# Three of seven triangular inversions from VectorE to GpSimd, and a new written order, in a delta-rule attention with an MLP mixer

## The chip, the cores and the metric

One core of one Trainium2 chip. The metric is the time of one execution on the device in microseconds, as the median of several runs. Inputs lie in the chip's memory (HBM) at the start, the output at the end.

## The reference

Two blocks in a row, all in fp32. The first is delta-rule attention, a recurrence over 768 positions for each of 4 batches x 8 heads with head dimension 48; the second mixes tokens and then channels with two small MLPs.

```python
# q, k, v: (4, 8, 768, 48), beta: (4, 8, 768)
k_n = k / (norm(k) + 1e-6)
for t in range(768):
    y[t] = q[t] @ state
    state = state + beta[t] * outer(k_n[t], v[t] - k_n[t] @ state)
x = y as (4, 768, 384)                       # heads side by side
h = relu(x.T @ w_tok1) @ w_tok2              # 768 -> 256 -> 768
u = x + h.T
out = u + relu(u @ w_ch1) @ w_ch2            # 384 -> 1536 -> 384
```

## The kernel before

**Units and rounds.** The sequence is cut into chunks of 64 positions, and two chunks make a unit: 6 units a batch, 24 in all (u = 0 to 23), 48 chunks (t = 0 to 47). Inside a chunk the recurrence becomes matrix products once the strictly triangular matrix of key products (times beta) of each head has been turned into the inverse of the identity plus it. The kernel inverts the 32 x 32 diagonal blocks of that matrix on a vector engine and joins the blocks to 64 x 64 with matmuls. Several units are inverted together, so that the 128 partitions hold 128 blocks: round 0 is units 0 to 3, round 1 units 4 and 5, rounds 2 to 5 four units each (6 to 9, 10 to 13, 14 to 17, 18 to 21), round 6 units 22 and 23.

**Jobs.** Every part of the work is a Python generator, a job, that records a few instructions at each step:

- `k`u loads keys and queries, `p`u (prep) makes norms, scales and masks (L497 mask times scale into `mb`, L514 scaled keys, both on GpSimd from u=4 on), `v`u loads the values and scales them (L411, L414 on GpSimd).
- `c`u and `d`u (grams): the key and query products of a unit's two chunks on TensorE (p_g, L440), which VectorE takes out of PSUM with the mask (L443, into `gm`).
- `t`u (to_parts): from u=6 on, four DMAs (L608) write the unit's 32 x 32 blocks to a tile in HBM, `n_dram`, from where `i` loads them in another layout, one block a partition.
- `i`r (invert): step 0 is one load (L655), steps 1 to 30 are one multiply (L661, into `sub`) and one add (L666, into `x`) each, step 31 sets the diagonal to one (L671) and stores the result to `w_dram` (L685).
- `f`u (from_parts): four DMAs (L633) bring a unit's inverted blocks back into `gm`.
- `j`u (join): VectorE transposes a block (L734), TensorE multiplies (p_z L748, p_x L751 and L767), ScalarE takes it out.
- `r`t (recur): the recurrence of a chunk: p_k (L790), rest on VectorE (L797), p_y and p_w (L810, L814), w_t on ScalarE (L820), p_s and p_y (L828, L829), the new state on VectorE (L837). Each chunk needs the state of the one before.
- `m`b (mixer): the MLPs of batch b, most of TensorE's work: p (L986), p_h (L999), p_ut (L1009), p_c (L1066) for batch 0, p_r (L958) for the others, and p_o (L1088).
- `w`n: pieces of the weights, loaded over SP (L271), scaled on ScalarE (L277, L278), shifted on VectorE (L280) and added on GpSimd (L284, unsigned integers); differences of weights on VectorE (L299, and `s`, L899).
- `x`, `z`, `Y`: matmuls of zeros whose results nobody reads, one narrow, one wide, eight small ones.

**Order.** Nothing reorders the instructions of an engine: a string, `order`, says which job makes its next step, and each engine's queue, SP's queue of DMAs too, runs in the order in which the steps were recorded. An engine waits at the head of its queue for semaphores. `i3*2` in the string means two steps of the fourth round's inversion.

**Engines and memories.** PE is TensorE, DVE VectorE, ACT ScalarE, POOL GpSimd. All DMAs are issued from SP. The inversions of all seven rounds run on VectorE.

Of the kernel before, what the change touches and what calls it, by code (L numbers as in the profile page):

```python
# [23 lines left out]
def kernel(  # L24
# [614 lines left out]
    def invert(rnd):  # L639
# [14 lines left out]
        else:  # L654
            nc.sync.dma_start(out=x, in_=xins.pop(rnd)[0:n])  # L655
        yield
        for s in range(1, m - 1):
            w = m - 1 - s
            tmp = work.tile([128, HB * HB // 4], FP32, name="sub")
# [1 line left out]
            nc.vector.tensor_tensor(  # L661
                out=tmp, in0=y[:, :, 0:s, s : s + 1].to_broadcast([n, k, s, w]),
                in1=y[:, :, s : s + 1, s + 1 : m].to_broadcast([n, k, s, w]),
                op=ALU.mult,
            )
            nc.vector.tensor_tensor(  # L666
                out=y[:, :, 0:s, s + 1 : m], in0=y[:, :, 0:s, s + 1 : m], in1=tmp,
                op=ALU.add,
            )
# [492 lines left out]
    order = """
    w10 x*4 z w10*2 z w1*4 k1*3 z k1*3 z b p1 z p1 k0*6 p0*2 b*2 p1 w2 p0*5 p1*2
    w10 p0*2 z w3 w2 c0*3 p0 w3*2 d0*2 w3 c0 p1 c0 d0*3 k2*3 v1 p1*2 w18 k2*2 p1*2
    c1*2 d1 k2 p2*2 c1 t0 d1 c1*2 d1*3 t0 p2*8 c2*2 w2 d2 c2*3 Y d2 w2 k3*6 p3 d2*2
    p3 d2 t1*3 x p3*7 c3 k4*5 k7 w13 w18*2 d3*2 v1*2 v0*2 c3*3 v0 c3 d3*3 t0 p4*2
    t2*3 x t3*2 p4*2 x t3 i0*2 w13 p4*2 w18 w17*2 i0 k4 i0*9 p4 i0*2 p4*2 c4 k8
    c4*3 w13*2 w6*2 k5*2 v0 k6 k5*2 i0*2 d4*2 k5 x z d4*3 c4 z*2 p5*2 k5 t4 p5 h0
    h1 h0 w8*2 h1 Y i0 f0 Y p4 f1 h2*2 p5*3 f0*2 w6 h0*5 k6*5 p6 z f2*2 k8*3 p5 w6
    p5 p3 p5 j0*3 f1*2 h1*5 j0*2 w8*2 w17 f2 h2*3 v0 t4*2 w17 r0*5 p6 h2*2 c5*2 v1  # L1170
    w11*2 j1 p5 k7*2 c5 k7 c5 r0 c5 r0*2 w14*2 v1 w11*2 k7*2 p7 d5*5 r1*5 w14*2
    p6*2 t5 j1 t5*2 r1*2 j1 j2 p7 h3*2 r1*3 p6*3 i1*2 r2*5 k8*2 f3*2 w9 k9*3 j1*2
    v2*2 i1*3 j2*2 r2*2 f3 i1*2 p6*3 w16 v2 w16*3 r2*2 h3 r2 i1 d6 r3*5 i1*2 w9*3
    v2 d6 h3 v2 w0 h3*2 r3 h3 d6*2 w0 d6 j3 c6*5 r3*4 w0 j2 w0 p8*2 j2 r4 p8 r4*4
    k9*3 j3*2 r4*2 i1*2 w24 i1*2 p7*7 r4 c7 r4 r5*5 k10 p9 k10 p9 c7 r4 c7*3 i1
    w5*2 p7 r5*2 w24*3 r5*3 j3*2 i1 r6*4 w26 v3*5 p9 k11 r6 d7*5 w26*3 p8*3 t6*2
    r6*2 w5*2 p8*4 v4*2 t6 i1 r6*3 h5*2 h4*2 k10*2 f4*3 c8*2 k10 p10 w28*2 c8*2 r7
    c8 r7*3 d8*4 p9 d8 w28 h4*5 p9 t6 r7*2 j4 w28 p9*3 r7*2 p9 w7 d9 w7 v4*2 f5*2
    w27*2 w7*2 d9*4 c9*2 f5 c9*3 t7*2 t8 r7*2 t7*2 j4*2 v4 p10*2 h5 r8*3 w29 t8*3
    w29 w27*2 r8*2 w29*3 j4*2 r8 w22*4 t9*4 r8*3 p10 h5*2 k11 p9 r8 h5 r9 h5 j5  # L1180
    r9*4 w4 i2*2 p10 i2*2 v5 i2 v5 w19 m0 r9 k10 j5 p10 i2 p10 v5 i2*2 w15 w4 v5*2
    w4 r9*2 i2 m0 v7 k11 j5 i2 k11*2 r9 v7 j5 p10 i2 r10 v7 i2 w15*2 i2 k12 r10*3
    w15 r10 r9 m0 j5 r10*3 i2*3 r10 p10 d10 c10*3 w25 i2 c10 d10*2 w19 k12 w4 k11
    r11*3 k12*2 w19 k12 i2 r11 r10 m0 r11 i2 r11*2 d10 Y i2*3 r11 w12 r11 i2*2
    k12*3 Y w19 w21 v6 i2 v6 i2*2 m0 i2 k12 i2*2 k12*2 w12 v6 i2*2 Y v6*2 m0*2 v7
    p12*2 m0*2 c10 m0 p11*2 f6 w21 p11 f6*2 m0*2 w12*2 f7*2 m0 f7 w21 p10 m0 p11*2
    d10 w21 m0 p12 m0 j6*2 f6 p11 j6 f8*2 w25 m0 f7 f8 w23 f8 p11 j7*3 w25 p12 m0
    w25*2 r12*2 v7 r12*3 j8*2 w31 r12 t10 w23*2 t10 j8 f9*2 m0 w23 r12 r13 w23 w32
    f9 k12 r13*2 t10*2 r13 f9 p12 p11 w31*3 r12 w30 k13 p11*2 k13 m0 r13*2 d11 k13
    d11 c11*2 r13 w32*3 r13*2 d11 w30 r13 w20*2 c11 k13*2 c11*2 w30*2 r14*2 k13 d11  # L1190
    k13 d11 r14*3 p12*2 w29 m0*4 w20*2 v8 r14 k13 d12 r14 c12 d12 c12 d12 p13 c12
    d12*2 k13*2 r14 p13*2 r14*2 m0 k13*2 v8*2 r15 w23 c12*2 w25 r15*4 p12 p13*2 v8
    w33 t11 j9 m0*2 w31 r15 p13*2 t11 t12 k14*2 m0 k14 m0*2 w31 r15 m0 r15 p13
    r15*2 c13*2 w31 k14*2 d13 c13 t11 d13 c13 d13 r16 d13 r16 c13 k14 d13 w33*2 v8
    w33 w27 k14 w27 t12*3 w33 k14 t13 r16*3 w33 m0*2 j9 w27 m0*2 t11 w25 j9 r16
# [7 lines left out]
    v11*3 r20 j11*2 m0*2 p15*2 k16*2 r20*2 m0 r20 c15 p15 d15*3 c15 j12 v11 p16 k16
    r20 d15 c15 p16*2 r21*2 c15 k16 c15 r21*2 r20 p16 r21 d15 f13 m0 p16*2 s r21*2
    m0 r21*2 j12 v11 r22*2 t14 r22*3 r21 m0 j12 r22*2 k17 p16 d16*2 s*2 c16 r22*2
    k17*3 m0 d16 k17 r22 k17 c16 k17*2 t15 k17*3 d16*2 c16 r23*2 c16*2 p17*3 r23
    p17 r23 t14 p17 k17 v12 r23 m0*2 p17 m0*2 s r23 p17 t14 r23 t15*2 m0*2 s v12
    c17 d17 c17*2 d17 t16 c17*2 d17*2 r23*2 d17 t16 m0*2 s*2 t16*2 m0 t14 v12*3 t15
    s t17 s*2 t17*3 m0*2 f12 m0*2 f13 i4 k18 j13 k18*2 m0*2 i4*3 p17 p16 m0 j13*2
    i4*4 m0*2 k18*2 i4*2 f13 r24*3 k18 r24*2 j13 k18*2 p18*2 k18 p18 r24 i4*2 r24  # L1210
    v14 m0 k18 m0*2 i4*3 m0*2 i4 k18*2 m0 i4 r24 r25*3 p18 r25 i4*2 v14*2 m1*2 v14
    p18 k19 i4 r25 k19 m1*3 k19 r25 m1 r25 i4*3 k19 i4 k19*3 r25 i4 v13*2 i4 v13*2
    i4*3 v13 k19 i4 m1 p18 i4*2 m1 p18 k19 r25*2 m1 k19 m1 p19 m1 r26 j13 p18 d18
    r26*2 d18 k19 r26*2 p19*2 m1*3 k19 r26 m1*3 f14*3 d18 c18*2 d18 r26*3 m1*5 c18
    r27*2 f14 c18 f17 r27*2 r26 r27 m1 p19 d18 j14 v14 m1*2 f15 r27 m1 r27 p19 f16
    j14 c18 f15*2 j14 r27*3 p19 m1*3 j15*2 f17 f16 p19 v15 j15 f16 k20*4 r28*4
    k20*2 m1*3 d19 r28*3 s m1 s k20*4 v15 s*2 r28 c19 d19*3 j16 c19*2 r28*2 d19
    r29*2 p19 c19 f16 k20 r29*2 f17 r29 v15*2 m1*2 k20 p20*2 c19 p20 m1*2 p20 f15
    m1*3 t18 r29 p20 k21 m1 r29 m1*3 p20 m1 k21*4 r29 m1*2 r29*2 p20 k21*3 m1 k21
    m1*3 k21 j16*2 t18 v15 k21 r30*5 k21 m1*3 r30 c20*3 p21*2 c20*2 t18 d20 r30  # L1220
    v16*2 t19 r30*2 p20 p21*2 r30 d20*3 r31*4 d20 r31*3 m1*2 p21*3 t19*3 r31*2 m1*2
# [57 lines left out]
```

## Time and profile before

| | us |
|---|---|
| median of 3 runs | 641.08 (639.05, 641.08, 644.09) |
| the profiled execution | 638.03 |
| its span, from first to last instruction | 636.3 |

| engine | busy us | share of the span | instructions |
|---|---|---|---|
| PE (matmuls) | 606.3 | 95% | 9132 |
| PEld (weight loads, beside PE) | 529.0 | 83% | 9132 |
| DVE | 447.3 | 70% | 1132 |
| ACT | 259.5 | 41% | 631 |
| POOL | 108.7 | 17% | 146 |

An fp32 matmul leaves two records, a transpose one. Rows of groups in the profile give the line, engine, operation, out<-in with partitions x elements and the count; behind the bar stand the busy time in us, the mean ns of one, and the engine's idle time just before them with what ended it. Rows of the timeline give the start in us, the length in us, engine, line, operation, and how many equal ones were merged.

### The profile page before, as it was taken

To read this page: it belongs to the slowest core of one execution; us is meant where nothing else is said; L and a number is where in the kernel's file an instruction comes from. 1 tells how busy PE (TensorE), PEld (TensorE's weight loads), DVE (VectorE), ACT (ScalarE), POOL (GpSimd) and SP (SyncE) were. 2 spreads that over 40 slices of the span, in tenths; PEclk is the share of its full clock that TensorE was granted. 3 is DMA by queue.
4 is the path that set the end of the run, shared out by engine and by line. 5 is a ranking of instruction groups with operands and counts; after the bars stand their busy time and mean duration, and the time that the engine had idled before them with its cause. 6 is when DMAs were issued, how large, how long until landed. Compare 5 with 4: busy or idle time off the path is not lost.

```text
span 636.3 us, 21488 instructions
## 1 busy us (share of the span) xinstructions
PE 606.3 (95%) x9132; PEld 529.0 (83%) x9132; DVE 447.3 (70%) x1132; ACT 259.5 (41%) x631; POOL 108.7 (17%) x146
## 2 busy tenths in 40 slices
...
GB/s 201 131 145 170 138 133 206 151 111 155 104 111 60 92 110 92 81 131 79 92 103 101 13 94 49 66 10 38 2 54 2 27 2 0 26 1 26 1 26 26
DMA packets 135776, 50.27 MB, mean 79 GB/s; under 512 B 114656, under 2 KB 130144, under 8 KB 135680
## 3 DMA queue, kind: packets, MB, share of 16 engines
...
q14 instruction: 24, 0.20, 0.1%
...
## 4 chain that ended last, share of the span: by engine, by line
PE 81%; DVE 7%; ACT 5%; DMA 3%; issue 2%; SPq 1%; POOL 0%; DVEq 0%; ACTq 0%; POOLq 0%
PE p_o L1088 26%; PE p_r L958 19%; PE p_c L1066 7%; PE p L986 5%; PE p_h L999 5%; PE p_k L790 3%; PE p_s L828 3%; PE p_g L440 3%; PE p_y L810 3%; DMA d<-in_moe_w_ch_dram 1%; PE p_z L748 1%; PE p_ut L1009 1%; PE p_w L814 1%; DVE sub L661 1%; PE p_y L829 1%
## 5 line engine op out<-in xcount | busy, mean ns | idle before, releaser
L1088 PE MATMUL p_o<-wc,r 128*128 128x192 f32 x720 | 125.8, 329 | 0.6 <-ACT u_t L1013 0.6
L1088 PEld LDWEIGHTS p_o<-wc,r 128*128 128x128 f32 x720 | 116.7, 190 | 2.7 <-ACT u_t L1013 1.1
L970 DVE TENSOR_TENSOR r<-r,p_r 128x512 f32<-128x512 f32 x90 | 59.7, 684 | 39.9 <-PE p_r L958 38.8
L1017 DVE TENSOR_TENSOR xb<-xb,p_o 128x192 f32<-128x192 f32 x84 | 29.3, 350 | 59.5 <-PE p_o L1088 59.3
L967 ACT COPY r<-p_r 128x512 f32<-128x512 f32 x54 | 31.5, 584 | 91.4 <-PE p_r L958 89.8
L666 DVE TENSOR_TENSOR x<-x,sub 128x84 f32<-128x84 f32 (+24 forms) x178 | 59.6, 335 | 6.1
L661 DVE TENSOR_TENSOR sub<-x 128x84 f32<-128x84 f32 (+24 forms) x178 | 58.4, 328 | 7.1 <-DMA x<-n_dram 2.8
L1066 PE MATMUL p_c<-u_t,wc 128*128 128x256 f32 x216 | 51.2, 387 | 0.2 <-ACT u_t L1013 0.2
L1088 PE MATMUL p_o<-wc,s 128*128 128x192 f32 x288 | 50.5, 329 | 0.3 <-DVE xb L1017 0.3
L414 POOL TENSOR_TENSOR v_st<-v_st,nrm 128x384 f32<-128x384 f32 x24 | 20.6, 859 | 174.6 <-DMA v_st<-in_v_dram 140.7
L1088 PEld LDWEIGHTS p_o<-wc,s 128*128 128x128 f32 x288 | 46.8, 190 | 1.2 <-DVE xb L1017 0.6
L820 ACT COPY w_t<-p_w 128x192 f32<-128x192 f32 x48 | 15.3, 319 | 73.2 <-PE p_w L814 72.5
L1066 PEld LDWEIGHTS p_c<-u_t,wc 128*128 128x128 f32 x216 | 39.6, 190 | 5.9 <-ACT u_t L1013 0.4
L974 ACT ACTIVATE r<-r 128x512 f32<-128x512 f32 x54 | 33.8, 630 | 25.6 <-DVE r L970 25.3
L440 PE MATMUL p_g<-kq 48*64 48x128 f32 (+1 forms) x704 | 38.3, 290 | 3.3 <-ACT kq L509 3.3
L497 POOL TENSOR_TENSOR mb<-mask_c,cs 128x512 f32<-128x512 f32 x20 | 21.0, 1050 | 114.1 <-DVE gm L443 45.1
L842 ACT ACTIVATE xb<-p_y 64x192 f32<-64x192 f32 x96 | 31.1, 324 | 21.3 <-PE p_y L829 10.5
L958 PE MATMUL p_r<-u_t,wc 128*128 128x128 f32 x288 | 38.5, 277 | 0.0
L958 PE MATMUL p_r<-t_d,wc 128*128 128x128 f32 x288 | 37.2, 280 | 0.0
L443 DVE TENSOR_TENSOR gm<-p_g,mb 128x512 f32<-128x512 f32 x44 | 29.4, 683 | 10.0 <-PE p_g L440 7.2
L986 PE MATMUL p<-xb,w 128*128 128x384 f32 x96 | 35.6, 513 | 0.0
L958 PEld LDWEIGHTS p_r<-u_t,wc 128*128 128x128 f32 x288 | 35.3, 192 | 0.3
...
## 6 DMA issues: line engine op xcount, KB each, us to landing
...
v_st<-in_v_dram SPq DMA_DIRECT2D x96, 48.0 KB, 2.5
...
kst<-in_k_dram SPq DMA_DIRECT2D x64, 48.0 KB, 3.2
...
```

What stands on the lines that cost most here:

```text
L440: nc.tensor.matmul(p_g[PAR[i ^ cc], p], kqt[f, p, cc, 0], kqt[f, p, cc])
L661: nc.vector.tensor_tensor(out=tmp, in0=y[:, :, 0:s, s : s + 1].to_broadcast([n, k, s, w]), in1=y[:, :, s : s + 1, s + 1 : m].to_broadcast( ...
L666: nc.vector.tensor_tensor(out=y[:, :, 0:s, s + 1 : m], in0=y[:, :, 0:s, s + 1 : m], in1=tmp, op=ALU.add,)
L842: nc.scalar.mul(y[:, :, D * i : D * i + D], p_y[PAR[1 - i]], 1.0 if c else -1.0)
L958: nc.tensor.matmul(p[:, i], pieces[i // width][:, at : at + 128], f[f"u{n}"], start=first and i == 0, stop=True, skip_group_check=True,)
L967: nc.scalar.copy(o, p)
L970: nc.vector.tensor_tensor(out=o, in0=o, in1=p, op=ALU.add if sign > 0 else ALU.subtract)
L974: nc.scalar.activation(o, o, ACTF.Relu)
L986: nc.tensor.matmul(p_1[dh], piece_of(w1, c, 0)[:, dh * 128 : (dh + 1) * 128], xb[:, c], start=(c == 0), stop=(c == NCH - 1),)
L999: nc.tensor.matmul(p_h, piece_of(w2, j, c * 128)[:, c * 128 : (c + 1) * 128], r1[j], start=(j == 0), stop=(j == NDH - 1),)
L1066: nc.tensor.matmul(p_c[:, k], piece_of(wc1, cb, f * 128)[:, f * 128 : (f + 1) * 128], u_t[:, cb], start=(cb == 0), stop=(cb == NCB - 1),)
L1088: nc.tensor.matmul(p, a[:, m], wc2[:, m, j], start=(start and i == 0), stop=(i == NM - 1), skip_group_check=True,)
```

## The change

In rounds 3, 4 and 5 (the fourth to the sixth) the 30 multiplies and 30 adds of the inversion are issued to GpSimd in place of VectorE. The load, the setting of the diagonal and the store stay where they were. The order is written anew from the first word to the last; the jobs and their steps are the same, but for the matmuls of zeros: 9 `x`, 16 `z` and 9 `Y` in place of 8, 10 and 6.

```diff
@@ invert @@
             nc.sync.dma_start(out=x, in_=xins.pop(rnd)[0:n])
         yield
+        solver = nc.gpsimd if rnd in (3, 4, 5) else nc.vector
         for s in range(1, m - 1):
             w = m - 1 - s
             tmp = work.tile([128, HB * HB // 4], FP32, name="sub")
             tmp = tmp[0:n, 0 : k * s * w].rearrange("b (k s w) -> b k s w", k=k, w=w)
-            nc.vector.tensor_tensor(
+            solver.tensor_tensor(
                 out=tmp, in0=y[:, :, 0:s, s : s + 1].to_broadcast([n, k, s, w]),
                 in1=y[:, :, s : s + 1, s + 1 : m].to_broadcast([n, k, s, w]),
                 op=ALU.mult,
             )
-            nc.vector.tensor_tensor(
+            solver.tensor_tensor(
                 out=y[:, :, 0:s, s + 1 : m], in0=y[:, :, 0:s, s + 1 : m], in1=tmp,
                 op=ALU.add,
             )
             yield
@@ order, the stretch of the fourth round @@
-    t13*2 s w29 t13 w23 j9 r16*2 i3 p14 r16 w33 p14 m0 j9 v10*2 r17*2 k14 r17*2 v10
-    r17 p14 v10 p14 v9 k14 p14 k15*2 i3 p14 m0*2 i3 m0 i3*3 r16 m0 i3*2 m0*2 k15
-    i3*3 k15*2 i3 v9 k15*2 i3 r17*2 m0*2 k14 v9 i3 m0 i3 m0*4 i3*5 k14 p14 r17*2 i3
-    m0*2 v9*2 k15 m0*4 i3 m0 r18 d14 r18 k15*3 p15 i3*3 r17 i3*2 r18*2 k15 r18 m0
-    i3*5 m0*5 f11 f10 r18 f10*2 f11 c14 d14 f12 c14 d14 c14 d14 r18*2 f11 v10 r18
...
+    r16*5 m0*3 t13*3 w33*2 m0 p12 k14 w33 w27 i3*3 w31 f9 w25 i3*2 k14 j9 v9*2 w33
+    k14*2 m0 k14*3 m0*4 v9 k14 m0 k14 w31 i3 m0*2 j9 m0 r16 i3*2 r16 i3*4 m0*2 i3*2
+    r16*3 v9*2 j9 i3 p14 r17*3 i3 r17*2 i3*2 v10*2 i3 p14*4 i3*2 m0 r17 p14 i3 j9
+    i3*4 k15*4 k14*2 i3 m0*5 r17*2 i3 r17 k15 r17 m0*6 r18 k14 p14 d14 r18 d14 k15
+    r18 k15*2 r18*2 d14 v10 c14*5 d14 k15*3 d14 k15 r18*2 i3*3 t14 v10*2 p15 m0*2
+    t14*2 p14 r18*2 m0*4 i3 r19 p15*2 r19*4 v11 m0*2 p15*3 r18 m0*2 s m0 s k16*3
+    t14 r19 m0*2 f10*3 f11*2 j10 m0*3 r19 f10 r19*2 f11 k16*4 j10*2 k16 p15 f12 k16
```

More of the change, by code (lines that the diff above doesn't have):

```diff
@@ L1169 @@
[L1169 to L1189, printed above, removed]
@@ L1203 @@
[L1203 to L1221, printed above, removed]
@@ new lines @@
+    r3*4 k9*2 i1*2 j2 v2*2 p8 r4*4 j2 r4 p8 w0*4 j3*2 r4*2 p7 i1*2 k10*2 p7*3 k7
+    p7*3 r4*3 r5*2 i1 r5*3 v3 p9 v3*2 c7*3 i1 r5 p9 w5*3 r5 c7*2 w24*3 w5 w24 r5*3
+    j3*2 i1 d7 k10 p8 r6*4 v3*2 p9 r6 k10*3 d7*4 p8*2 w26*4 t6*4 r6*2 p8*5 r6*3
+    h5*2 i1 h4*2 p7 f4*2 f5 c8*4 f4 c8 d8*4 f5 p10 d8 p10 v4*5 r7*5 w28*4 p9 h4*5
+    p9 j4 r7*2 p9*4 w7 r7 w7 r7 c9*3 r7 w7*2 c9 d9*2 p10 d9 t7*2 c9 t7*2 d9*2 w27*3
+    t8*2 r8*2 t8*2 j4*2 w29 w22 f5 h5 w29*2 j4*2 r8*3 w27 w29*2 w22*3 r8 p10*2 t9*3
@@ new lines @@
+    r8 t9 z r8*2 Y w4 i2 h5*4 j5 w4*2 r9*4 w29 v5 z r8 r9*3 i2*4 v5 x r9*2 j5 r9 j5
+    i2 v5*2 i2*3 p10*2 i2 k12 w19*3 w4 z i2 w15*3 r10 m0*2 i2 r10*3 v5 r10 j5 z i2
+    j5 p10 i2*3 p10 r10 m0 r10*2 w25 k12*3 k11 k12 v6 m0 d10 r10 r11*4 i2*2 r10
+    k12*2 w15 k12 p12 Y r11*3 w12 k12 i2*4 k11*3 v7 c10*2 v7 v6 k11 i2*7 w19 d10 i2
+    d10*2 w12 k12*3 r11*2 m0*2 k11 c10 m0 w21 v6*2 i2*2 m0*2 v6 m0 p12 d10 m0*2 p10
+    w12*2 p11*2 w25*3 m0*2 p11 c10*2 p12 p11*2 w27 w21*2 p11 m0 w21 v7*2 f6*2 m0*2
@@ new lines @@
+    f6 j6*2 s f7 w23 f7 j6 f7*2 w23 m0 j7 w23 f6 j7 w25 m0 j7 w32 f8*3 w32 v7 f9 j8
+    w23 r12*5 w23*2 j8 w32 w29 j8 r12 p11 r12 f9 p11*3 r13*4 t10 r13 r12 p12 m0
+    r13*2 d11 c11*2 p12 p9 w30*3 w32 d11 r13*2 c11*3 w30 f9 d11 w23 d11 w20 r14*2
+    d11 r14*2 t10 r14 r13 w31 p12*2 t10*2 w31*3 k13 m0*4 r14 d12 w25 c12*2 k13*3
+    r14 k13*6 w20*2 k13*2 f8 r14*3 d12*2 c12 d12 c12 p13 v8 p13 v8 r15*3 p13 r15
+    w20 m0 r15*2 v8 w33 v8 d12 c12 j9 t12 r15 m0*2 p13*2 t12*2 p13*2 r15 p13 d13
+    c13 t12 t11 c13*2 d13 t11*2 r15*2 c13*2 d13*3 w27 m0 v8 t11 w33 t13 w33 w31
@@ new lines @@
+    c17 d17 c17*2 d17*2 s*3 m0*2 t16 m0 t17*4 v12 f12 s m0 f13 m0*2 i4*4 m0 i4*2
+    f13 i4 s*2 m0*7 i4 f13 v12*2 i4*7 k18*5 m0 k18*2 i4 j13 m0*4 i4*2 k18 p18 k18
+    v14 k18 v14 f13 j13 m0*2 j13 r24*5 m1 m0 m1 r24*2 i4*2 j13 r25 p18 k18 i4*3 k18
+    r25*2 p18 r25*2 v13*2 p18*2 k19 v13 r24 k19*2 i4*4 k19 m1 i4*4 j13 m1 v14 v13
+    r25 v13 p18 m1*2 p18 r25*2 k19*7 v14 i4 r25 k19 f14*2 m1*3 f15 m1*3 r26 f14 r26
+    f14 d18 r26*3 r25 m1*2 f15 v14 m1*3 r26 d18 m1 c18 d18 c18 d18 r26 c18 r26*2
@@ new lines @@
+    p19 d18 m1*4 r26 m1 r27 f15 c18 f16 r27*3 m1 r27 c18 m1*2 r27 f16*2 p19*2 m1
+    j14 r27 f15 j14 p19*2 j14 j15 r27 k20 m1 r27 p19*2 m1 p18 m1 r27 j15 j16 r28*4
+    j15 r28 m1 r28*2 d19 m1 s*2 c19 k20*3 d19 k20*3 c19 d19 c19 d19*2 r28*2 m1*2
+    r29 c19 r28 r29*3 k20 s k20*3 s c19 p20 m1 f16 r29 p20*2 m1*4 p20 r29*2 m1*2
+    p20*2 v15 m1*7 t18 v15*2 k20 m1 p20 r29*2 k21 v15 f17 k21 p19 j16 r30*3 r29 j16
+    k21*4 t19 v15 m1 t19 r30*2 m1*3 r30*2 m1 r30 c20 p20 d20 c20 r30 d20 c20 d20*2
+    t18 k21*3 r31 d20 v16 r30 c20 r31*2 f17 r31*2 m1*3 r31 m1*2 r31 m1*3 k21 p21*2
@@ new lines @@
+    v16 p21 k21*2 m1 t18 m1 t18 c20 m1 p21 t19 f17 v18 t20*2 m1 v16 p21*2 t20*2 p21
+    m1*3 k22*2 m1 r31*2 k22 v16 c21 d21 c21*2 d21 t19 c21*2 d21 r32 d21*2 t21*2 j17
+    r31 t21 r32*3 m1*2 t21 m1 v16 r32 v18 p21 m1*4 i5*2 k22*2 m1*4 j17 m1*2 j17
+    k22*2 f17 k22*4 m1*4 r32*2 m1*3 r32*2 p22 m1*3 r33 p22*3 i5*2 r33*2 i5*2 k22
+    v18 r33 j17 r32 r33*3 p22 k23*3 i5 k23*2 m1*4 k23 v17 i5 p22 r33 i5*2 m1 r33
+    p22 m1*4 k23 m1*3 i5 j17 k23 v17*3 i5 m1*2 i5 m1*2 p23 m1*3 d22 m1*2 r34*2 d22
+    r34 v17 r34*2 m1*4 k23 m1*2 k23*3 r33 v18 r34 d22 c22 v18 c22 d22*2 c22 i5
```

64 lines of the change are left out of this document (30 added, 34 removed).

## The prediction

> **What bounds the kernel now.** The page's engine rows come first, then the busy time by stretches, then who waited for whom.
>
> ```profile
> PE 606.3 (95%) x9132; PEld 529.0 (83%) x9132; DVE 447.3 (70%) x1132; ACT 259.5 (41%) x631; POOL 108.7 (17%) x146
> ...
> 0.00:40.00 40.00, 27.19 (x288) 18.87 (x289) 28.95 (x87) 25.85 (x65) 11.72 (x23) 0.87 0.94 166
> 40.00:120.00 80.00, 68.12 (x1902) 56.95 (x1900) 64.26 (x157) 61.31 (x167) 41.99 (x52) 0.92 0.66 154
> 120.00:160.00 40.00, 39.09 (x610) 28.19 (x608) 28.23 (x71) 21.77 (x53) 14.94 (x18) 0.99 0.59 143
> 160.00:460.00 300.00, 299.55 (x4747) 263.31 (x4742) 244.46 (x632) 102.05 (x252) 38.22 (x53) 1.00 0.34 75
> ```
>
> Each stretch row gives its length, then busy time of PE, PEld, DVE, ACT and POOL, then granted clock and DMA. From 160 to 460 us, where the three rounds that move to GpSimd run, PE is busy 299.55 of 300 us while DVE has 244.46. DVE is four fifths full there, and PE does not wait for it. PE's idle time lies in the first 120 us: 12.81 and 11.88 us.
>
> ```profile
> PE p_t L505 <- DMA pads<-in_q_dram: 6.4, 1, 6.4
> PE p_w L814 <- DVE rest L797: 3.5, 5, 1.3
> PE p_g L440 <- ACT kq L509: 3.3, 4, 1.4
> ```
>
> These longest waits lie in that first part, but for 0.4 us of the second. Taking work off DVE in rounds 3 to 5 can therefore give back at most 0.45 us directly. What can change the time is whether a round on GpSimd still ends before PE needs it, and what the new order does in the first 120 us.
>
> **The change part by part.** An inversion is 30 steps of a multiply (sub) and an add (x), each dependent on the one before, on s(31-s) elements a partition: 4960 for each of the two kinds in a round, 165.3 in the mean. By the page's groups
>
> ```profile
> L666 DVE TENSOR_TENSOR x<-x,sub 128x84 f32<-128x84 f32 (+24 forms) x178 | 59.6, 335 | 6.1
> L661 DVE TENSOR_TENSOR sub<-x 128x84 f32<-128x84 f32 (+24 forms) x178 | 58.4, 328 | 7.1 <-DMA x<-n_dram 2.8
> ```
>
> DVE loses 3 x 30 x (0.335 + 0.328) = 60 us, from under PE's busy time, so this brings 0. On DVE the fourth round (i3) lasts from 180.16 to 206.44 us, 26.3. Beside it stand the other ends of that round's chain: evicted grams, loading, and the first join matmul.
>
> ```profile
> 169.81 1.27 DVE L443 TENSOR_TENSOR gm<-p_g,mb 128x512 f32<-128x512 f32 x2
> ...
> 176.47 0.34 SPq L655 DMA_DIRECT2D x<-n_dram  x1
> ...
> 180.16 0.20 DVE L661 TENSOR_TENSOR sub<-x 128x30 f32<-128x30 f32 x1
> ...
> 206.23 0.21 DVE L666 TENSOR_TENSOR x<-x,sub 128x30 f32<-128x30 f32 x1
> ...
> 209.27 6.06 SPq L633 DMA_DIRECT2D gm<-w_dram  x10
> ...
> 214.50 0.45 DVE L734 STREAM_TRANSPOSE t<-gm 128x256 f32<-128x256 f32 x1 [0.77 <-DMA gm<-w_dram]
> ...
> 217.79 0.69 PE L748 MATMUL p_z<-t,gm 32*32 32x32 f32 x32
> ```
>
> So i3 takes 10.35 us from the last gram's eviction to the first step, 26.3 of inversion, 8.5 to the transposed join tile (214.95), and 2.8 us were to spare before PE came for it.
>
> The cost on GpSimd comes from its own rows; minimum, median and maximum in ns stand after the count.
>
> ```profile
> L414 POOL TENSOR_TENSOR v_st<-v_st,nrm x24: 827/829/1372, 52.4 to 473.6; 128x384 f32<-128x384 f32 x24
> L411 POOL TENSOR_TENSOR nrm<-nrm,eps x24: 191/200/647, 52.2 to 471.6; 128x8 f32<-128x8 f32 x24
> L497 POOL TENSOR_TENSOR mb<-mask_c,cs x20: 1038/1042/1204, 29.0 to 377.6; 128x512 f32<-128x512 f32 x20
> L284 POOL TENSOR_TENSOR wc<-w_f,d x24: 1001/1012/1167, 6.7 to 171.5; 128x384 uint32<-128x384 uint32 x24
> L284 POOL TENSOR_TENSOR w<-w_f,d x10: 727/812/1166, 6.0 to 114.9; 128x256 uint32<-128x256 uint32 x6, 128x384 uint32<-128x384 uint32 x4
> ...
> 284.64 0.20 POOL L411 TENSOR_TENSOR nrm<-nrm,eps 128x8 f32<-128x8 f32 x1
> 284.93 0.83 POOL L414 TENSOR_TENSOR v_st<-v_st,nrm 128x384 f32<-128x384 f32 x1
> ```
>
> With one operand broadcast, 200, 829 and 1042 ns at 8, 384 and 512 elements give 0.185 us + 1.67 ns an element. With two dense operands, 727 ns at 256 and 1001 at 384 give 0.18 us + 2.14 ns. The last two rows show a dependent instruction starting some 0.08 us after the end of the one it needs. The multiply has a broadcast operand, so 30 x (0.185 + 0.276) = 13.8 us; the add has two dense ones, nearest to L284, so 30 x (0.18 + 0.354) = 16.0; 60 gaps of 0.08 make 4.8. That is 34.6 us a round, with 32.4 (all at the broadcast rate) and 36.8 (all dense) as the ends. Its shapes of short rows aren't in this trace; I take no more for them.
>
> By the Trainium skill, page "GPSIMD Engine Reference", section "Elementwise — side-by-side cycle accounting", an elementwise add of two fp32 tensors took 4497 ns for 2048 elements, 2.2 ns each, the rate of the L284 rows; the L414 row is faster than that. By this rate alone the round would be an estimated 36.8 to 37.5 us.
>
> GpSimd's queue adds what stands between the steps: in i3 the scaling of v9 (0.2 + 0.83) and a mask product for u=14 (1.04), 2.3 us with gaps; in i4 one v scaling, 1.3; in i5 two of them, a mask product and a key scaling, 4.6. Nothing of these is needed earlier than it comes, except the mask product, which DVE's gram eviction for u=14 waits for; PE has its next use of that bank only at the join.
>
> Then the two engines get in each other's way.
>
> ```profile
> 196.25 0.83 POOL L414 TENSOR_TENSOR v_st<-v_st,nrm 128x384 f32<-128x384 f32 x1
> 196.31 1.01 DVE L661 TENSOR_TENSOR sub<-x 128x220 f32<-128x220 f32 x1
> 197.35 0.90 DVE L666 TENSOR_TENSOR x<-x,sub 128x220 f32<-128x220 f32 x1
> ...
> L661 DVE TENSOR_TENSOR sub<-x x30: 182/348/409, 256.9 to 281.2; 128x30 f32<-128x30 f32 x2, 128x58 f32<-128x58 f32 x2, 128x84 f32<-128x84 f32 x2, 128x108 f32<-128x108 f32 x2
> ```
>
> A DVE instruction with both inputs in SBUF took 1.01 us beside a GpSimd one, while in the fifth round no step took over 0.41. With GpSimd computing without a break, each such DVE instruction waits for a GpSimd one and then holds up the next. Between the first and last step the new order has ten of them in i3 (weight differences of 0.4 us, halves of 0.55; 4.7 in all), seven in i4 (3.8) and twenty in i5 (7.7). If each holds up GpSimd by its length less the gap, that is 3.9, 3.2 and 6 us; if none, 0. I take half: 2, 1.6 and 3.
>
> The Trainium skill, "SBUF — State Buffer", section "Who interferes with whom", states just this: a Vector instruction with two SBUF inputs and a GpSimd one that reads SBUF exclude each other for a whole instruction. It speaks against the change; the trace agrees with its 1.01 us.
>
> So i3 lasts 34.6 + 2.3 + 2 = 38.9 us (34.7 to 43.0), i4 37.5 (33.7 to 41.3) and i5 42.2 (37.0 to 47.4).
>
> What PE has to do meanwhile is counted in the two orders between the last gram matmul of a round and its first join matmul.
>
> ```profile
> 247.33 1.29 DVE L443 TENSOR_TENSOR gm<-p_g,mb 128x512 f32<-128x512 f32 x2 [1.11 <-issue]
> ...
> 251.84 0.34 SPq L655 DMA_DIRECT2D x<-n_dram  x1
> ...
> DMA to landing us min/median/max: 3.6/3.7/4.2
> ...
> 293.62 0.69 PE L748 MATMUL p_z<-t,gm 32*32 32x32 f32 x32
> ...
> 323.60 0.68 DVE L443 TENSOR_TENSOR gm<-p_g,mb 128x512 f32<-128x512 f32 x1
> ...
> 394.00 0.69 PE L748 MATMUL p_z<-t,gm 32*32 32x32 f32 x32
> ...
> L1088 PE MATMUL p_o<-wc,r 128*128 128x192 f32 x720 | 125.8, 329 | 0.6 <-ACT u_t L1013 0.6
> L1066 PE MATMUL p_c<-u_t,wc 128*128 128x256 f32 x216 | 51.2, 387 | 0.2 <-ACT u_t L1013 0.2
> ```
>
> An instruction costs PE its group's busy time over its count, 175 ns for p_o and 237 for p_c (two records a matmul). In i3 the new order has 18 more p_o, three more transposes and some small ones: 4.2 us on top of the 48.0 from 169.81 to 217.79, so 52.2. The chain needs 10.35 + 38.9 + 8.5 = 57.7: PE waits 5.5 us. The point from which it waits at all is an inversion of 33.3 us. In i4 it has 18 more p_c and eight more p_r, 4.6 us, so 46.3 + 4.6 = 50.9; the load can land at 255.5, 8.2 after the eviction, and the chain needs 8.2 + 37.5 + 8.5 = 54.2: 3.3 us (turning point 34.2). In i5 it has 48 p_o fewer, 70.4 - 8.4 = 62.0, against 10.35 + 42.2 + 8.5 = 61.1: nothing. By the bounds the three give 0.4 to 21 us: i3 0.4 (its load up to 1 us earlier) to 9.7, i4 0 to 7.1, i5 0 to 4.3. The wait begins on SP: the store of the inverse now waits for GpSimd, and behind it in SP's queue stand a few rows of v, k and grams that nobody needs yet, then the loads of the inverse (L633) for the join; they take the place that they had, so the 8.5 us stay. Behind PE's wait everything on PE is queued, and it goes to the end undiminished.
>
> The new order also has ten warming steps more: six wide (z) and one narrow (x) of two records each, and three (Y) of eight small ones.
>
> ```profile
> L225 PE MATMUL p_warm<-warm 128*128 128x512 f32 (+1 forms) x36 | 15.0, 563 | 1.1 <-DVE warm L112 1.1
> L235 PE MATMUL p_warm<-warm 64*64 64x128 f32 x48 | 3.6, 274 | 0.0
> ...
> 98.00:108.00 10.00, 8.04 (x151) 5.88 (x146) 5.32 (x21) 5.96 (x17) 4.18 (x6) 0.66 0.83 225
> 116.00:120.00 4.00, 3.53 (x92) 3.32 (x83) 3.76 (x12) 2.35 (x6) 0.35 (x1) 0.65 1.12 234
> ```
>
> That is 14 x 0.42 + 24 x 0.075 = 7.7 us of PE work. It stands ahead of r11, the recurrence that began at 119 us, in a stretch where PE idles 24.7 us, and DVE's, ACT's and GpSimd's work ahead of that point differs by under 2 us between the orders. I put this part at 0, from -4 (the clock rows: 8.04 us at 0.66 and 3.53 at 0.65 would shrink by 2.7 and 1.2 at full clock) to +3 (four wide steps of two records each at 15.0/36 = 0.42 us, at 100 to 118 us, where PE is nearly full).
>
> The sum: the profiled execution took 638.0 us (span 636.3), so 638.0 + 5.5 + 3.3 + 0 = 646.8. The median of the runs shown, 641.1, lies 3.1 above it; on that scale the forecast is 650 us.
>
> **The rivals.** *The early part wins.* The warming steps keep the clock at 1 near 100 and 117 us and save the 3.9 us above, and an inversion stays under 33.3 us, so that nothing waits: 634.1, or 637. For it: the clock rows. Against it: 32.4 us of bare steps leave 0.9 for GpSimd's other 2.3 us. It decides where the steps' rate is that of L414 and the load comes a microsecond earlier. *The rounds fit: the move changes nothing.* Waits of at most 2 us, early part even: 638 to 640, or 641 to 643. For it: PE's added work between grams and join in both rounds; against it the dense rate. *Twice held up.* All steps at L284's rate and every DVE instruction in the way: 9.7 + 7.1 + 4.3 gives 659.1, or 662. It decides where DVE's two-input instructions come one by one between GpSimd's steps rather than in a row.
>
> **How the numbers follow.** Forecast (4 to 15 us more) 0.5; rounds fit 0.25; held up twice 0.15; early part wins 0.1. The likeliest gives 650. The range is 639 to 662: down to most of the second rival and the nearer half of the first, up to the third. One per cent, 6.4 us, is about what a measurement of this kernel tells from no change. Slower by more than that: most of the forecast and the third rival, 0.57; within it 0.38; faster by more 0.05.
>
> **What would show it.** Right: GpSimd's busy time rises by about 90 us and DVE's falls by 60; the multiply's and add's means on GpSimd near 460 and 530 ns; PE waits of some microseconds before the first join of u=10 and u=14, none before u=18; the stretch to 120 us as long as before. Wrong: steps at 380 ns or less, PE 100% busy from 160 to 460 us, or r11 beginning microseconds earlier or later than 119.

## The result and the profile after

| | before | after |
|---|---|---|
| median, us (4 runs each) | 641.15 (639.05 to 644.09) | 658.59 (657.34 to 659.93) |
| the profiled execution, its span | 638.03, 636.3 | 659.93, 658.2 |

The ratio is 1.0272, with a 95% interval of 1.0235 to 1.0309: 17.4 us longer. In what follows a kernel's time is given as its excess over before, its ratio less one times 641.15, since the runs did not all share one chip; the changed kernel's is +17.4 (15.1 to 19.8). The profiled execution of before is shorter than any of its four runs and that of the changed kernel is the longest of its four, so the 21.9 us between the two profiles overstate the change.

The engine row of the changed kernel's page, and busy time by stretches (length, PE, PEld, DVE, ACT, POOL, granted clock, DMA):

```profile
PE 625.8 (95%) x9170; PEld 541.8 (82%) x9170; DVE 397.3 (60%) x952; ACT 260.5 (40%) x631; POOL 201.7 (31%) x326
...
0.00:40.00 40.00, 31.66 (x321) 21.29 (x322) 28.32 (x86) 26.09 (x64) 10.44 (x22) 0.92 0.74 149
40.00:120.00 80.00, 69.31 (x1748) 57.15 (x1746) 54.41 (x130) 57.95 (x157) 40.67 (x50) 0.83 0.63 143
120.00:160.00 40.00, 38.07 (x539) 25.90 (x540) 35.01 (x90) 20.20 (x50) 13.50 (x15) 1.00 0.62 145
160.00:460.00 300.00, 292.46 (x4654) 255.36 (x4653) 182.69 (x421) 99.93 (x250) 133.52 (x234) 0.98 0.35 78
```

Between 160 and 460 us PE, which had 0.45 us of idle time, now has 7.54, while DVE fell from 244 to 183 us. PE's busy time over the whole span rose by 19.5 us, from 606.3 to 625.8: 12.8 of them are warming steps (31.4 us in all, 18.6 before), and the rest is on the other matmuls, of which there are as many as before; the granted clock is lower, 0.83 from 40 to 120 us where it was 0.92. The longest waits of PE (total, times, longest) are two from the early part and two new ones:

```profile
PE p_g L440 <- ACT kq L509: 6.8, 4, 5.8
PE p_w L815 <- DVE rest L798: 5.6, 5, 3.2
PE p_z L700 <- DVE gm L443: 4.7, 1, 4.7
PE p_z L749 <- DVE t L735: 4.2, 2, 3.8
```

The two groups that moved, now on POOL, and the timeline around the ends of the fourth round (i3) and the fifth (i4); lines of the code behind the new one are one higher than before:

```profile
L667 POOL TENSOR_TENSOR x<-x,sub 128x30 f32<-128x30 f32 (+14 forms) x90 | 48.8, 542 | 7.1
L662 POOL TENSOR_TENSOR sub<-x 128x30 f32<-128x30 f32 (+14 forms) x90 | 45.8, 509 | 27.2 <-DMA x<-n_dram 20.9
...
186.79 0.24 POOL L662 TENSOR_TENSOR sub<-x 128x30 f32<-128x30 f32 x1 [3.63 <-DMA x<-n_dram]
225.56 0.26 POOL L667 TENSOR_TENSOR x<-x,sub 128x30 f32<-128x30 f32 x1
225.85 0.34 SPq L686 DMA_DIRECT2D w_dram<-x  x1
229.09 0.40 SPq L633 DMA_DIRECT2D gm<-w_dram  x1
233.37 0.45 DVE L735 STREAM_TRANSPOSE t<-gm 128x256 f32<-128x256 f32 x1 [6.46 <-DMA gm<-w_dram]
233.87 0.31 PE L749 MATMUL p_z<-t,gm 32*32 32x32 f32 x8 [3.81 <-DVE t L735]
...
269.60 0.26 POOL L662 TENSOR_TENSOR sub<-x 128x30 f32<-128x30 f32 x1 [11.03 <-DMA x<-n_dram]
305.50 0.26 POOL L667 TENSOR_TENSOR x<-x,sub 128x30 f32<-128x30 f32 x1
306.00 0.83 POOL L414 TENSOR_TENSOR v_st<-v_st,nrm 128x384 f32<-128x384 f32 x1
306.86 0.36 DVE L798 TENSOR_TENSOR rest<-p_k,v_st 128x192 f32<-128x192 f32 x1 [3.86 <-POOL v_st L414]
307.27 0.34 PE L815 MATMUL p_w<-rest,gm 64*64 64x48 f32 x1 [3.22 <-DVE rest L798]
```

i3 takes 39.0 us and PE waits 3.81 us for its result at the join of u=10. i4 takes 36.2 us, but here PE does not wait at the join: it waits 3.22 us ahead of r26, for the scaling of v13 that stood behind i4's last add in POOL's queue. Behind each wait the clock is low:

```profile
230.00:234.00 4.00, 0.19 (x12) 0.13 (x10) 0.63 (x3) 0.00 (x0) 0.99 (x2) 1.00 0.34 53
234.00:238.00 4.00, 4.00 (x43) 3.96 (x41) 2.02 (x5) 1.38 (x4) 0.00 (x0) 0.57 0.47 81
...
304.00:308.00 4.00, 0.78 (x29) 0.73 (x32) 1.14 (x3) 0.38 (x1) 3.61 (x9) 0.78 0.36 129
308.00:312.00 4.00, 4.00 (x77) 3.91 (x70) 3.39 (x12) 0.74 (x2) 0.99 (x2) 0.50 0.34 63
312.00:316.00 4.00, 4.00 (x72) 3.65 (x70) 2.39 (x6) 1.77 (x5) 0.00 (x0) 0.86 0.35 54
```

The 4 us at 0.57 lose 1.7 us of full-clock time; 0.50 and 0.86 lose 2.0 and 0.6. The idle 3.8 and 3.2 us thus cost some 5.5 and 5.8.

The other place is the first 60 us. The chain that ended last passes here through two wide warming steps, which stand between the matmuls that follow the first inversion (i0) and take 2 us each, at half clock:

```profile
45.38 3.62 PE p_z L700 x64
49.00 2.00 PE p_warm L225 x2
51.01 1.85 PE p_z L700 x32
52.85 1.31 PE p_x L713 x32
54.16 2.00 PE p_warm L225 x2
...
44.00:48.00 4.00, 2.62 (x50) 2.65 (x51) 3.90 (x5) 2.04 (x6) 0.36 (x1) 0.50 1.24 239
48.00:52.00 4.00, 4.00 (x42) 2.43 (x41) 1.46 (x5) 2.28 (x7) 1.29 (x2) 0.50 0.47 84
52.00:56.00 4.00, 4.00 (x52) 2.77 (x50) 1.33 (x4) 2.35 (x7) 1.98 (x3) 0.50 0.00 0
56.00:60.00 4.00, 4.00 (x113) 3.62 (x111) 0.45 (x1) 2.88 (x8) 3.86 (x6) 0.86 0.44 114
```

The loss is there when the recurrence begins: w_t of r0 (L821) starts at 62.2 us in place of 54.8. Part of it arises ahead of the two steps: i0's first step starts 2.2 us later, and the first matmul behind i0, p_z, at 45.4 us in place of 42.1. In VectorE's queue the shift of a weight (L280) stands in front of the grams that i0 needs, and it waits 1.1 us for ScalarE. First the changed kernel, then before:

```profile
26.63 0.36 DVE L280 TENSOR_SCALAR w_f<-d 128x384 uint32<-128x384 uint32 x1 [1.12 <-ACT d L277]
32.17 0.19 DVE L662 TENSOR_TENSOR sub<-x 128x28 f32<-128x28 f32 x1
...
29.98 0.19 DVE L661 TENSOR_TENSOR sub<-x 128x28 f32<-128x28 f32 x1
```

r11 begins at 131.3 us in place of 119.0; in the profile of e8 (below), whose early part is the same, it begins at 128.0, so this pair of profiles shows more of a loss than the medians do.

### The profile page after: what moved, and what is told of

Same layout as the page of the kernel before. It is cut to its first block, busy times and chain, and to the rows that moved or that the text cites. A ratio compares the mean times of both kernels' runs of the same rounds, so it can differ in the third digit from the quotient of the medians.

```text
span 658.2 us, 21574 instructions
## 1 busy us (share of the span) xinstructions
PE 625.8 (95%) x9170; PEld 541.8 (82%) x9170; DVE 397.3 (60%) x952; ACT 260.5 (40%) x631; POOL 201.7 (31%) x326
## 4 chain that ended last, share of the span: by engine, by line
PE 71%; POOL 9%; DVE 6%; DMA 4%; ACT 3%; issue 3%; SPq 3%; DVEq 0%; POOLq 0%; ACTq 0%
PE p_o L1089 21%; PE p_r L959 20%; POOL x L667 4%; POOL sub L662 4%; PE p_h L1000 4%; PE p_c L1067 3%; PE p L987 3%; PE p_k L791 3%; PE p_g L440 3%; PE p_y L811 2%; PE p_s L829 2%; PE p_warm L225 2%; DVE sub L662 1%; DMA x<-n_dram 1%; PE p_z L749 1%
## 5 line engine op out<-in xcount | busy, mean ns | idle before, releaser
L1089 PE MATMUL p_o<-wc,r 128*128 128x192 f32 x720 | 128.4, 332 | 0.6 <-ACT u_t L1014 0.6
L1089 PEld LDWEIGHTS p_o<-wc,r 128*128 128x128 f32 x720 | 118.3, 192 | 2.6 <-ACT u_t L1014 1.1
L662 POOL TENSOR_TENSOR sub<-x 128x30 f32<-128x30 f32 (+14 forms) x90 | 45.8, 509 | 27.2 <-DMA x<-n_dram 20.9
L667 POOL TENSOR_TENSOR x<-x,sub 128x30 f32<-128x30 f32 (+14 forms) x90 | 48.8, 542 | 7.1
L440 PE MATMUL p_g<-kq 48*64 48x128 f32 (+1 forms) x704 | 38.9, 291 | 6.8 <-ACT kq L509 6.8
L284 POOL TENSOR_TENSOR wc<-w_f,d 128x384 uint32<-128x384 uint32 x24 | 24.5, 1026 | 56.4 <-ACT d L278 20.4
L440 PEld LDWEIGHTS p_g<-kq 48*64 48x64 f32 (+1 forms) x704 | 29.5, 142 | 10.7 <-ACT kq L509 8.7
L821 ACT COPY w_t<-p_w 128x192 f32<-128x192 f32 x48 | 15.2, 316 | 54.7 <-PE p_w L815 54.3
L959 PEld LDWEIGHTS p_r<-u_t,wc 128*128 128x128 f32 x288 | 36.2, 196 | 0.3
L959 PEld LDWEIGHTS p_r<-t_d,wc 128*128 128x128 f32 x288 | 34.1, 191 | 1.0
```

The lines of the kernel that those rows point to most:

```text
L440: nc.tensor.matmul(p_g[PAR[i ^ cc], p], kqt[f, p, cc, 0], kqt[f, p, cc])
L662: solver.tensor_tensor(out=tmp, in0=y[:, :, 0:s, s : s + 1].to_broadcast([n, k, s, w]), in1=y[:, :, s : s + 1, s + 1 : m].to_broadcast([n, ...
L667: solver.tensor_tensor(out=y[:, :, 0:s, s + 1 : m], in0=y[:, :, 0:s, s + 1 : m], in1=tmp, op=ALU.add,)
L959: nc.tensor.matmul(p[:, i], pieces[i // width][:, at : at + 128], f[f"u{n}"], start=first and i == 0, stop=True, skip_group_check=True,)
L1089: nc.tensor.matmul(p, a[:, m], wc2[:, m, j], start=(start and i == 0), stop=(i == NM - 1), skip_group_check=True,)
```

## The experiments

The theory: two separate losses, the new order's early part and the two long rounds. The rivals: the order alone, GpSimd alone, or losses that hide each other.

**e1: the new order, all rounds on VectorE.**

```diff
-        solver = nc.gpsimd if rnd in (3, 4, 5) else nc.vector
+        solver = nc.vector
```

> The changed order with all seven inversions on VectorE. Theory (two separate losses: the new order's first 131 us, and PE held up at the joins of u=10 and u=14 by GpSimd's long rounds): the two stretches in which PE stands idle and the slow clock behind them, about 7 + 4 us, go; the early loss of 8 to 12 us stays: 646 to 651 us. Rival A (the order alone costs everything): 657 to 660. Rival B (GpSimd's rounds alone cost everything): 640 to 643.

Measured: 698.1 us, ratio 1.0887 (1.0845 to 1.093), +57. All three guesses missed. PE's waits, and the first and last start of the multiplies of i3 and i4 together:

```profile
PE p_o L1089 <- DVE xb L1018: 13.3, 5, 4.9
PE p_r L959 <- DVE r L971: 10.5, 2, 7.5
...
L662 DVE TENSOR_TENSOR sub<-x x60: 191/350/416, 185.6 to 317.3; 128x30 f32<-128x30 f32 x4, 128x58 f32<-128x58 f32 x4, 128x84 f32<-128x84 f32 x4, 128x108 f32<-128x108 f32 x4
```

The new order spreads a round's steps over some 40 us of other work, as GpSimd needs them. On VectorE, in that order, i3 lasts 41.5 us and i4 41.7, longer than on GpSimd, though their instructions take 20 us; and what stands behind a step that waits is late for PE. The order is written for the engine, so the two halves of the change cannot be priced one at a time; the cut has to go by place.

**e2: the old order, rounds 3 to 5 on GpSimd.** The solver line is that of the change, the order string that of before.

> The order of before, with rounds 3 to 5 on GpSimd and nothing else changed. Theory: the rounds last 39, 36 and 43 us as in the changed kernel; the old order leaves 48.0, 46.3 and 70.4 us from the last gram's eviction to the first join matmul against chains of 58, 53 to 55 and 62 us, so PE waits 10 + 7 + 0 us and loses some 3 more to the clock behind it: 657 to 662 us. Rival (VectorE's relief pays for it, or only the new order's early part costs): 641 to 645.

Measured: 670.8 us, ratio 1.048 (1.0445 to 1.0514), +30.8, beyond the theory's 657 to 662. The stretch of the three rounds, and one row of VectorE's waits there:

```profile
160.00:460.00 300.00, 280.48 (x4317) 243.42 (x4315) 176.01 (x392) 90.18 (x226) 130.74 (x231) 0.97 0.34 74
...
DVE rest L798 <- POOL v_st L414: 15.3, 3, 10.8
...
230.20 0.45 DVE L735 STREAM_TRANSPOSE t<-gm 128x256 f32<-128x256 f32 x1 [8.52 <-DMA gm<-w_dram]
```

The rounds last 38.7, 38.4 and 40.1 us, near what was expected, but PE idles 19.5 us, and mostly not where it was expected to: for the joins' own matmuls it waits 2.7 us. In i3 the recurrence waits for scaled values that stand between GpSimd's steps: VectorE stands still 10.8 us for them, of which PE feels 2.8 us. Its longest wait, 6.0 us at 231 us, does come from i3's end: the `rest` that PE needs stands in VectorE's queue behind the transpose for the join, which waits 8.5 us for the inverse. The budget between grams and join sees neither what else GpSimd's queue holds nor what stands in VectorE's queue behind the join's transpose.

**e3 and e4: the two orders cut at r11.** In e3 the words of the order of before run up to the last r11, then follow what is left of the changed order, with rounds 3 to 5 on GpSimd; in e4 the other way round, with all rounds on VectorE.

```diff
-    z x*2 w1*2 w10 x w10*2 k1 w10 k1*2 z k1*3 p1 b Y p1 k0*6 p0*2 v1 z*2 v0 Y*2 b*2
+    w10 x*4 z w10*2 z w1*4 k1*3 z k1*3 z b p1 z p1 k0*6 p0*2 b*2 p1 w2 p0*5 p1*2
...
```

> The order of before up to the last step of r11, from there the changed order (what was already done is left out of it), rounds 3 to 5 on GpSimd. Theory: r11 starts at 119 us again in place of 131, the waits at the joins of u=10 and u=14 stay: 646 to 651 us. Rival (the chain of the third and fourth round sets the time, and the early loss is hidden in its waits): 656 to 660.

> The changed order up to the last step of r11, from there the order of before, all inversions on VectorE. Theory: the early loss alone, 8 to 12 us on top of before: 648 to 653 us. Rival (the loss of the first 131 us is made up later, in PE work that fills what were gaps): 641 to 644.

Measured: e3 651.4 us, ratio 1.0153 (1.0125 to 1.0181), +9.8; e4 648.5, ratio 1.0119 (1.0098 to 1.014), +7.6. Taking the early part away saves 7.6 us, adding it alone costs 7.6: the losses do not hide each other, and 9.8 us belong to what lies behind r11. They include a wait that only the joining of the two orders makes: 2.5 us at 130 us, ahead of p_h, which neither whole order has; that the two parts add up to 17.4 to the decimal is chance. From 160 to 460 us PE idles 6.3 us in e3 and 0.6 in e4, a row each:

```profile
160.00:460.00 300.00, 293.69 (x4652) 257.08 (x4651) 184.85 (x422) 100.05 (x250) 132.05 (x232) 0.98 0.36 77
```

```profile
160.00:460.00 300.00, 299.36 (x4874) 261.34 (x4873) 243.57 (x622) 107.23 (x264) 44.29 (x59) 1.00 0.37 80
```

**e5 and e6: the warming steps.** e5 moves the two wide steps of 49.0 and 54.2 us ahead; e6 takes out ten, these two among them.

```diff
-    ... p5 z d4 t4 z w6 w8*2 i0 h0*2 ... p5*3 z w14 h2*2 f1 f0 h0*2 z h0*3 ...
+    ... p5 z d4 t4 z*3 w6 w8*2 i0 h0*2 ... p5*3 w14 h2*2 f1 f0 h0*5 ...
```

> The changed kernel with two of its wide warming steps (z), which ran at 48.9 and 54.1 us between the end of the first inversion and the first recurrence step, moved ahead, to 40.5 us, where TensorE is idle for 4 us. Theory (warming steps lie on the path there, 2.1 us each at half clock): 4 us less, up to 8 if the clock also comes back earlier: 650 to 655 us. Rival (the slow clock from 44 to 56 us comes from what lies between, and the steps run in its shade): 657 to 660.

> The changed kernel without ten warming steps: the six wide ones at 48.9, 54.1, 112.4, 115.1, 118.6 and 124.5 us, the narrow one at 67.2, the sets of eight at 58.9, 75.3 and 113.9, so that their number is that of before. Theory (the first two cost 2.1 us each on the path, the next three 2.7 together, the rest half of their 4.8): 6 to 9 us less, 649 to 653 us. Rival A (they stand in idle time, as the prediction had it): 657 to 660. Rival B (without them the clock is lower still): 661 or more.

Measured: e5 652.2 us, ratio 1.021 (1.0189 to 1.0232), +13.5; e6 652.9, ratio 1.0212 (1.0183 to 1.0242), +13.6. They save 3.9 and 3.8 us, each uncertain by some 3 us; the two wide steps are 4.0 us long. The other eight of e6 brought nothing more that these runs can tell; e6 fell short of its 6 to 9. Some 3.7 us of the early part are then not the warming steps. The traces show where they lie: in e5 and e6 w_t of r0 starts at 58.1 and 58.2 us, 3.4 later than before, and p_z behind i0 at 44.6 and 44.5, 2.5 later. So most of this part is lost ahead of p_z. The weight's shift in VectorE's queue ahead of i0 is the likely cause, but no run moved it, so this is not shown.

**e7: the scaling of the values on VectorE.**

```diff
+        scaler = nc.vector if u >= 9 else nc.gpsimd
-        nc.gpsimd.tensor_tensor(
+        scaler.tensor_tensor(
             out=nrm, in0=nrm, in1=eps[:, :, None].to_broadcast([128, NP, 2]), op=ALU.add
...
```

> The changed kernel with the scaling of the values of units 9 to 23 (an add and a multiply each) on VectorE in place of GpSimd. In the changed kernel the scaling of v13 stands behind the fourth round's (i4) last add in GpSimd's queue, and PE waits 3.2 us for it ahead of r26. Theory (that place in the queue is what costs in i4): this wait and the slow clock behind it go, 3 to 6 us less: 652 to 656 us. Rival (the join of u=14 waits for the inversion anyway, 8 us later, so the wait only moves there): 657 to 659.

Measured: 662.6 us, ratio 1.0381 (1.0346 to 1.0415), +24.4: slower than the change itself, against both guesses. PE's waits from 290 to 410 us:

```profile
PE p_w L816 <- DVE rest L799: 2.9, 2, 2.7
PE p_z L750 <- DVE t L736: 2.0, 1, 2.0
```

The wait ahead of r26 is down to 0.2 us, and the join of u=14 at once waits 2.0: the rival is right on the place, the inversion would have been late too, though not on the time. The 2.7 us are a new wait after 330 us, and VectorE's queue now stands still for v's transfers (9.2 us in three). These rows do not add up to 7 us, and the profiled execution (660.1 us) is the shortest of the four; the rest stays open.

**e8 and e9: shorter rounds.** e8 leaves steps out in rounds 3 and 4, e9 (`rnd == 3`) in one.

```diff
         for s in range(1, m - 1):
+            if rnd in (3, 4) and s >= 24:
+                yield
+                continue
             w = m - 1 - s
```

> The changed kernel with the last seven of the 30 steps of rounds 3 and 4 left out (part of the inversion is not computed), which shortens them from 39.0 and 36.2 us to some 31 and 29.7. Theory (PE waits from an inversion of 33.3 and 34.2 us upwards, and these two rounds are all that the move to GpSimd costs): both stretches of idle PE go, with the slow clock behind them: 8 to 10 us less, 648 to 651 us. Rival (half or more of the cost is in GpSimd's and VectorE's mutual hindrance and in the order, whatever the rounds' length): 653 to 658.

> The changed kernel with the last seven steps left out in round 3 alone (part of its inversion is not computed), which cut it and round 4 together by 10 us in the time. Theory (each round has its own wait, 3.8 us of idle PE in the third round and 3.2 in the fourth, and the slow clock after each): 5 to 7 us less than the changed kernel, about 650 to 652 where before has 639 to 641. Rival (the fourth round's wait only follows from the third's lateness, so both go): 646 to 648.

Measured: e8 645.1 us, ratio 1.0111 (1.0063 to 1.0158), +7.1; e9 652.5, ratio 1.0169 (1.012 to 1.0218), +10.8. With rounds of 30.7 and 30.0 us PE has no wait between 160 and 460 us:

```profile
160.00:460.00 300.00, 299.87 (x4839) 262.60 (x4832) 191.75 (x443) 105.78 (x263) 121.84 (x208) 1.00 0.35 79
```

Two rounds that end in time save 10.3 us, and leave +7.1, what e4 found for the early part. The third round's share is 6.6, the fourth's 3.7, each uncertain by some 4 us. In e9 the wait ahead of r26 stands at 3.1 us though i3 is in time, so it does not follow from the third round's; the rival falls.

**e10: the old early part and short rounds.** e3 with the edit of e8.

> The order of before up to the last step of r11, then the changed order, and rounds 3 and 4 without their last seven steps (part of the inversion is not computed). Theory (the early part and the two long rounds are the whole loss and add up, 7.3 + 10.2 us): the time of before within 2 us, 638 to 643. Rival A (they overlap, so that one of them makes up for the other): 645 or more. Rival B (the new order of the rest is itself better than the old one, and only hidden by the long rounds): 636 or less.

Measured: 639.05 us, ratio 0.9964 (0.9943 to 0.9986), -2.3. The two losses add up to the whole; with both gone, and part of GpSimd's steps as well, 2 us are even gained, too little for the second rival; no row here says where. The wait ahead of p_h is here too, 1.9 us.

**e11: the old order, the sixth round (i5) alone on GpSimd.**

```diff
-        solver = nc.gpsimd if rnd in (3, 4, 5) else nc.vector
+        solver = nc.gpsimd if rnd == 5 else nc.vector
```

> The order of before with round 5 alone on GpSimd. Theory by the prediction's budget (70.4 us from the last gram's eviction to the join of u=18 in the old order, a chain of 62 us): no wait, 639 to 642 us. Rival (what stands behind the steps in GpSimd's and VectorE's queues is late for the recurrence: the scaling of v17 and v20 and the setting of the diagonal): 645 to 650.

Measured: 644.6 us, ratio 1.0066 (1.0037 to 1.0094), +4.2, between the theory's range and the rival's. The join has no wait. PE's one long wait in the round is at 368 us:

```profile
362.22 0.70 POOL L667 TENSOR_TENSOR x<-x,sub 128x234 f32<-128x234 f32 x1
363.00 0.73 POOL L662 TENSOR_TENSOR sub<-x 128x228 f32<-128x228 f32 x1
363.81 0.68 POOL L667 TENSOR_TENSOR x<-x,sub 128x228 f32<-128x228 f32 x1
...
363.20 0.69 DVE L928 TENSOR_TENSOR t_c<-u_t 128x128 f32<-128x128 f32 x1
363.92 0.72 DVE L928 TENSOR_TENSOR t_c<-t_c,u_t 128x128 f32<-128x128 f32 x1
364.56 0.28 DVE L928 TENSOR_TENSOR t_d<-u_t 128x128 f32<-128x128 f32 x1
...
368.02 2.90 PE L1089 MATMUL p_o<-wc,s 128*128 128x192 f32 x12 [3.07 <-DVE xb L1018]
```

VectorE has a dozen differences (L928) and halves (L1041) in a row here, and the two that fall beside GpSimd steps take 0.69 and 0.72 us where the third needs 0.28. From 358 us to PE's wait, twelve of VectorE's instructions take 4.2 us more in all than the medians of the same ones before. The eviction behind them is late, and PE waits 3.07 us for it. So the cost is neither the budget's nor what the rival named: it is the two engines holding each other up, paid on VectorE. The Trainium skill ("SBUF — State Buffer", section "Who interferes with whom") says that a Vector instruction with two SBUF inputs contends with a GpSimd one that reads SBUF, over ports that are an exclusive lock; these rows, 0.69 and 0.72 us beside 0.28, agree.

**e12: more warming in the old order.** The kernel before, with five words more:

```diff
-    ... t7*2 j4*2 v4 p10*2 h5 r8*3 ... t9*4 r8*3 p10 ... r8 h5 r9 ...
+    ... t7*2 z j4*2 v4 p10*2 h5 z r8*3 ... t9*4 r8 z r8*2 p10 ... r8 h5 z r9 ...
```

The fifth stands ahead of the eighth step of r10.

> The kernel before with five more wide warming steps (z, 0.84 us of PE each at full clock), ahead of the second step of j4, the first and eighth of r8, the first of r9 and the eighth of r10 (94 to 116 us), where PE idles 0.36 to 0.54 us each and the granted clock falls to 0.52 to 0.66 behind. Theory (the prediction's upper bound, the clock stays at 1 and saves up to 4 us, the steps cost 0.3 to 0.5 us each on the path): 637 to 640 us where before has 639 to 641. Rival (the clock does not hang on these few microseconds and the steps are simply on the path): 642 to 645.

Measured: 640.2 us, ratio 0.9988 (0.996 to 1.0017), -0.8. The clock does come up, to 1.00 from 0.88 in this stretch:

```profile
80.00:120.00 40.00, 36.88 (x893) 27.18 (x894) 31.09 (x82) 27.79 (x74) 19.26 (x24) 1.00 0.69 161
```

Yet r11 begins at 118.7 us, 0.3 earlier. Ahead of the first added step this execution was 0.6 us behind, so some 0.9 us are gained: most of what the clock gives, the steps take. No version that computes everything beats the kernel before by more than this, and this is not clear of no change.

## Why the prediction was right and where it was wrong

**VectorE's relief brings nothing: right.** 62 us less of VectorE's work from 160 to 460 us, and no stretch of PE is better for it. The relief was also smaller: 50 us in place of 60 over the whole span. Some 7 of the other 10 are VectorE's other instructions with two inputs: L299 went from 409 to 486 ns in the mean, the halves `r<-r,s` (L1040, now L1041) from 549 to 606. Of these instructions 33 fall inside the three rounds, and there they take 4.4 us more than the medians of the same ones before. The prediction counted this only as time lost by GpSimd.

**The cost of a round: right, in part by luck.** Adding up, for each of the 60 instructions, the shortest of its three times gives 29.9 us against 13.8 + 16.0: 14.5 for the multiplies and 15.4 for the adds, so that two errors of 0.7 and 0.6 us cancel. The gaps are 0.078 us each, as taken. Above these 29.9, hindrance cost 2.7, 0.7 and 1.5 us in the three rounds (32.6, 30.6 and 31.4 of busy time) where 2, 1.6 and 3 were put down. The means of 509 and 542 ns hold that hindrance; without it they are 485 and 513, where 460 and 530 were put down. The rounds lasted 39.0, 36.2 and 43.4 us against 38.9, 37.5 and 42.2; i5's 5.9 us pause, in which GpSimd scaled v17 and v18 and waited 3.5 us for their transfers, was longer than the scaling put down for it, and i5 had the time.

**The wait behind i3: the place right, the size by luck.** 5.5 us of waiting were predicted and 3.8 found. PE's work between grams and join was 52.3 us, as reckoned (52.2); the chain was 56.1 in place of 57.7, because the first step came 9.0 us after the eviction, not 10.35, and the transposed tile 8.0 after the last step, not 8.5. The 1.7 us that are missing came back as slow clock, which the prediction did not have. e9 puts the whole at 6.6, uncertain by some 4.

**The wait behind i4: the size near, the place wrong.** 3.3 us at the join were predicted; 3.2 came ahead of r26. That the size is near is luck in part: the round was 1.3 us shorter than reckoned, and its first step came 9.5 us after the eviction, not 8.2. (The 4.6 us of added work come to 5.3 by the prediction's own price for p_c and the page's row for p_r, 38.5 us for 288; PE was busy 53.7 us there at a clock of 0.94, 50.5 of full-clock time where 50.9 were reckoned.) The step that failed is the sentence on GpSimd's queue, "Nothing of these is needed earlier than it comes, except the mask product": v13's scaling was needed 3.9 us earlier than it came. e7 shows that the join's wait stood right behind it, 2.0 us.

**No wait behind i5: right** for the changed kernel (0.3 us at the join of u=18).

**The slow clock after a wait: left out.** The prediction let PE's wait go "to the end undiminished"; the rows show the first grown by 0.45 of its length and the second by 0.8.

**The early part: wrong, and this step by itself put the centre some 8 us too low.** It was put at 0, from -4 to +3, and is 7.6 us by e3 and by e4. Its own sign of being wrong, r11 microseconds off 119, came true. Sums of work ahead of r11 were compared, and the ten warming steps were set against 24.7 us of idle time as a whole. What counts is where a step stands: two of the wide ones stood in the chain between i0 and r0, where PE had nothing idle, and cost their full length (e5, 3.9 us), 2 us each at half clock where 0.84 had been reckoned. The rest lies mostly ahead of these steps: the matmuls behind i0 begin later, which a comparison of sums of work does not see. The lower bound failed too: e12 has the full clock that it asked for and gains 0.8 us (2.6 at most by its interval) of 4.

**The sum.** Rounds 10.3 in place of 8.8, early part 7.6 in place of 0: with 641.1 that makes 659, and 658.6 was measured. The forecast's range held although one of its terms was outside its own bounds. The third rival, 662, came nearest in number but not in kind: no round was longer than foreseen by more than 1.2 us.
